# Loading the last two V tiles of a decode attention kernel in quarters

## The chip, the cores and the metric

The kernel runs on one core of a Trainium2 chip. The metric is the device time of one execution in microseconds (us). All runs quoted were in the fast state that the measuring reports. Inside that state the kernel before still shows two groups of times, which the experiments explain.

## The reference

One query per head attends to 8192 keys: 16 heads, head size 256, all in bf16.

```python
B, H, Sq, Sk, D = 1, 16, 1, 8192, 256
scores = jnp.einsum("bhqd,bhkd->bhqk", q, k) * D ** -0.5
p = softmax(scores, axis=-1)
out = jnp.einsum("bhqk,bhkd->bhqd", p, v)
```

K and V are 134 MB together (2 x 16 x 8192 x 256 x 2 bytes), and each byte is used once.

## The kernel before

Each partition holds 64 consecutive rows of K or V of a head, so a tile is [128, 64, 256] and one load is 4 MB. VectorE (DVE) and ScalarE (ACT) compute the scores from K. GpSimd (POOL) takes the maximum across partitions, ACT the exponential, and TensorE (PE) accumulates 64 matmuls with V, one for each row of a partition. After each head come "fill" matmuls whose result nobody reads: they keep PE busy.

```python
KV_BUFS=(3, 3), K_AHEAD=2, NV_CHUNKS_LAST=1, N_FILL=45, N_FILL_LAST=58
...
for h in range(H):
    if h + K_AHEAD < H:
        issue_k(h + K_AHEAD)
    vt = vpool.tile([P, NJ, D], bf16, name=f"vt{h}", tag="vt")
    nvc = NV_CHUNKS_LAST if h == H - 1 else 1
    vstep = (NJ + nvc - 1) // nvc
    for c in range(0, NJ, vstep):
        ce = min(NJ, c + vstep)
        nc.sync.dma_start(out=vt[:, c:ce, :], in_=v_r[h][:, c:ce, :])
    ...                                   # scores, maximum, exponential -> p_sb, lsum
    for j in range(NJ):                   # "value matmuls": oacc
        nc.tensor.matmul(oacc[:, :], lhsT=p_sb[:, j : j + 1], rhs=vt[:, j, :],
                         start=(j == 0), stop=(j == NJ - 1))
    nc.tensor.matmul(ssum[:, :], lhsT=ones_col[:], rhs=lsum[:])
    nfill = N_FILL_LAST if h == H - 2 else (N_FILL if h < H - 1 else 0)
    ...                                   # nfill matmuls of 512 columns: fill
```

The build sets the order on an engine, and it is not that of the source. In the trace of before, for instance, the fills of head 14 start at 294.74 us, the value matmuls of head 13 at 307.38 and those of head 14 at 316.15.

## Time and profile before

| | before |
|---|---|
| time, median (16 runs) | 341.15 us (339.4 to 341.6) |
| span of the profiled execution | 339.4 us |
| bytes read | 135.27 MB, 399 GB/s over the span |
| PE busy / DVE busy | 81% / 83% |

The first lines are from the page of the kernel before. PEclk is the clock granted to PE in tenths of full speed and DMA the busy share of the 16 DMA engines, each in 40 slices of the span; the last line is an issue group: line, queue, number of issues, size, median time from issue to landing.

```profile
PEclk9999958999999999999999999999999999999979
DMA  8999999999999999999999999999999999999300
...
vt<-in_v_dram SPq DMA_DIRECT2D x16, 4096.0 KB, 44.8
```

The DMA row is at 9 from slice 2 to slice 37 of 40 (421 to 450 GB/s): the kernel is bound by its loads, except in the last three slices. There the PEclk row drops to 7. (The 5 in slice 6 is there before PE has its first value matmuls, at 54.2 us here.) All 16 loads of V are single ones of 4 MB.

The next lines are the timeline of PE at the end: start, duration, engine, line and operation, what it writes and reads, how many, and the idle time before it with what ended it. L178 is the fills, L164 the value matmuls, L172 the sum.

```profile
294.74 12.71 PE L178 MATMUL fill<-qb,p 128*64 128x512 bf16 x58
307.38 7.15 PE L164 MATMUL oacc<-vt,p 128*1 128x256 bf16 x64
315.11 0.19 PE L172 MATMUL ssum<-lsum,ones_col 128*1 128x1 f32 x2 [0.58 <-ACT p L153]
316.15 7.15 PE L164 MATMUL oacc<-vt,p 128*1 128x256 bf16 x64 [0.85 <-DMA vt<-in_v_dram]
325.82 8.77 PE L164 MATMUL oacc<-vt,p 128*1 128x256 bf16 x64 [2.53 <-DMA vt<-in_v_dram]
```

These are heads 13, 14 and 15. The last two wait for V. Head 15 waits 2.53 us and then needs 8.77 us for what takes 7.15 us elsewhere. The next lines give windows of the tail: the window, its length, the busy time and number of instructions of PE, of PE's weight loads, of DVE, ACT and POOL, and in the last three columns the granted clock, the DMA share and GB/s.

```profile
310.00:314.00 4.00, 4.00 (x39) 3.09 (x37) 3.61 (x21) 0.00 (x0) 0.10 (x1) 1.00 0.97 418
318.00:322.00 4.00, 4.00 (x39) 3.09 (x37) 0.00 (x0) 0.00 (x0) 0.00 (x0) 1.00 0.12 49
322.00:326.00 4.00, 1.47 (x14) 0.87 (x13) 0.47 (x1) 0.00 (x0) 0.48 (x1) 0.97 0.04 17
326.00:330.00 4.00, 4.00 (x24) 2.55 (x23) 0.00 (x0) 0.00 (x0) 0.00 (x0) 0.60 0.00 0
```

From 318 us on only two, then less than one of the 16 DMA engines on average still move data (0.12, then 0.04), and PE stands waiting for it. Then the clock is 0.60 while the last head is computed.

### The profile page before, as it was taken

How to read it: one execution, taken by the hardware profiler on the slowest of the kernel's cores; microseconds unless marked ns; L12 is line 12 of the kernel's file. 1: busy time of each engine (PE TensorE's matmuls, PEld its weight loads, DVE VectorE, ACT ScalarE, POOL GpSimd, SP SyncE). 2: the span in 40 equal slices, each digit the busy share in tenths (PEclk: the TensorE clock that was granted, in tenths of full speed). 3: DMA queues.
4: the chain of work that ended last, by engine and by line, in shares of the span. 5: the costliest groups of instructions: out<-in, count | busy, mean ns of one | idle time of the engine just before them, and what ended most of it. 6: DMA issues, size and time to landing. Idle time of an engine off the chain costs nothing.

```text
span 339.4 us, 5929 instructions
## 1 busy us (share of the span) xinstructions
PE 274.2 (81%) x1744; PEld 162.8 (48%) x1744; DVE 281.3 (83%) x1297; ACT 183.5 (54%) x897; POOL 15.2 (4%) x36
## 2 busy tenths in 40 slices
PE   0008649999998989898989989879889798899874
PEld 0003226556564646455555646446365554556643
DVE  0998999993998989898989999796998969699000
ACT  0938575660937557392919385581927549093000
POOL 0000020100000000000000000000000000000000
PEclk9999958999999999999999999999999999999979
DMA  8999999999999999999999999999999999999300
GB/s 315 450 433 433 432 426 431 426 432 428 421 427 434 430 431 432 428 430 432 432 432 428 429 434 431 433 430 431 434 423 430 432 427 427 432 427 432 164 8 1
DMA packets 5727, 135.64 MB, mean 400 GB/s; under 512 B 1088, under 2 KB 1088, under 8 KB 1088
## 3 DMA queue, kind: packets, MB, share of 16 engines
q1 hardware_dynamic: 5184, 135.27, 93.0%
q8 instruction: 13, 0.21, 0.3%
q14 instruction: 18, 0.15, 0.1%
q0 software_dynamic: 512, 0.01, 0.1%
HBM read 135.27 MB, written 0.01 MB: 399 GB/s over the span
## 4 chain that ended last, share of the span: by engine, by line
DVE 50%; DMA 28%; PE 11%; issue 7%; POOL 1%; ACT 1%; SPq 0%; POOLq 0%; ACTq 0%; DVEq 0%
DVE kt L127 37%; DMA kt<-in_k_dram 28%; DVE kt L112 11%; PE fill L178 7%; PE oacc L164 4%; DVE scores L127 1%; POOL gmx L141 1%; ACT p L153 1%; DVE mx L139 1%; PE ssum L172 1%; DVE rs L90 0%; DVE nbias L145 0%; POOL out_dram L93 0%; POOLq L215 0%; SPq L73 0%
## 5 line engine op out<-in xcount | busy, mean ns | idle before, releaser
L127 DVE CUSTOM_DVE_ANT_0 kt<-kt,qb 128x256 bf16<-128x256 bf16 x592 | 205.8, 413 | 0.0
L119 ACT ACTIVATE kt<-kt 128x256 bf16<-128x256 bf16 x432 | 172.8, 401 | 26.9 <-DVE kt L112 21.1
L178 PE MATMUL fill<-qb,p 128*64 128x512 bf16 x688 | 157.0, 389 | 0.0
L164 PE MATMUL oacc<-vt,p 128*1 128x256 bf16 x1024 | 116.0, 275 | 10.6 <-DMA vt<-in_v_dram 10.6
L178 PEld LDWEIGHTS <-p 128*64 128x64 bf16 x688 | 76.1, 113 | 73.9 <-issue 6.7
L164 PEld LDWEIGHTS <-p 128*1 128x1 bf16 x1024 | 85.3, 85 | 43.1 <-DMA vt<-in_v_dram 13.4
L119 ACT ACTIVATION_READ_ACCUMULATOR kt<-kt 128x1 f32 x432 | 80.5, 186 | 0.0
L112 DVE TENSOR_TENSOR kt<-kt,qb 128x1024 bf16<-128x1024 bf16 (+2 forms) x48 | 62.3, 1343 | 13.7 <-DMA kt<-in_k_dram 13.7
L153 ACT ACTIVATE p<-scores,nbias 128x64 bf16<-128x64 f32 x16 | 5.6, 348 | 96.6 <-DVE nbias L145 67.4
L127 DVE DVE_READ_ACCUMULATOR2_ANT scores<- 128x1 f32 x592 | 45.0, 76 | 0.0
L172 PE MATMUL ssum<-lsum,ones_col 128*1 128x1 f32 x32 | 3.0, 164 | 49.8 <-ACT p L153 49.8
L172 PEld LDWEIGHTS ssum<-lsum,ones_col 128*1 128x1 f32 x32 | 1.4, 81 | 54.5 <-ACT p L153 54.1
L92 DVE TENSOR_SCALAR osb<-oacc,rs 1x256 bf16<-1x256 f32 x16 | 7.5, 470 | 23.7 <-PE oacc L164 23.3
L141 POOL PARTITION_ALL_REDUCE gmx<-mx x16 | 6.9, 431 | 283.6 <-DVE mx L139 283.6
L93 POOL DMA_DIRECT2D out_dram<-osb x16 | 8.1, 508 | 36.8 <-DVE osb L92 35.6
L145 DVE TENSOR_SCALAR nbias<-gmx 128x1 f32<-128x1 f32 x16 | 2.5, 154 | 8.6 <-POOL gmx L141 8.6
L90 DVE RECIPROCAL rs<-ssum 1x1 f32<-1x1 f32 x16 | 2.5, 155 | 5.6 <-PE ssum L172 5.5
L119 ACT ACT_TABLE_LOAD x1 | 1.3, 1283 | 8.1 <-DMA kt<-in_k_dram 8.1
L139 DVE TENSOR_REDUCE mx<-scores 128x1 f32<-128x64 f32 x16 | 3.5, 219 | 1.4
L153 ACT ACTIVATION_READ_ACCUMULATOR p<-scores,nbias 128x1 f32 x16 | 3.0, 186 | 0.0
L61 DVE MEMSET ones_col<- 128x1 f32 x1 | 0.1, 59 | 0.8 <-PEq L204 0.8
L204 POOL MEMSET const-float32-0.0<- 128x1 f32 x1 | 0.1, 98 | 0.2 <-issue 0.2
(3 smaller groups left out, 0.3 us busy)
## 6 DMA issues: line engine op xcount, KB each, us to landing
vt<-in_v_dram SPq DMA_DIRECT2D x16, 4096.0 KB, 44.8
kt<-in_k_dram SPq DMA_DIRECT2D x15, 4096.0 KB, 37.3
kt<-in_k_dram SPq DMA_DIRECT2D x4, 1024.0 KB, 9.9
qb<-in_q_dram SPq DMA_DIRECT2D x1, 1024.0 KB, 4.7
out_dram<-osb POOLq DMA_DIRECT2D x16, 0.5 KB, 6.6
```

Of the source, the lines that this page charges most:

```text
L90: nc.vector.reciprocal(rs[:], ssum[:, :])
L92: nc.vector.tensor_scalar_mul(o_sb[:], oacc[:, :], rs[:])
L93: nc.gpsimd.dma_start(out=out[0, h], in_=o_sb[:])
L112: nc.vector.tensor_tensor(out=kt[:, c0:c1, :], in0=kt[:, c0:c1, :], in1=qbb.to_broadcast([P, c1 - c0, D]), op=MULT,)
L119: nc.scalar.activation(kt[:, j, :], kt[:, j, :], mybir.ActivationFunctionType.Copy, accum_out=scores[:, j : j + 1],)
L127: nc.vector.tensor_tensor_reduce(out=kt[:, j, :], in0=kt[:, j, :], in1=qb[:, h, :], scale=1.0, scalar=0.0, op0=MULT, op1=ADD, accum_out=sc ...
L139: nc.vector.reduce_max(mx[:], scores[:], axis=mybir.AxisListType.X)
L141: nc.gpsimd.partition_all_reduce(gmx[:], mx[:], channels=P, reduce_op=bass_isa.ReduceOp.max)
L153: nc.scalar.activation(p_sb[:], scores[:], mybir.ActivationFunctionType.Exp, bias=nbias[:], scale=scale, accum_out=lsum[:],)
L164: nc.tensor.matmul(oacc[:, :], lhsT=p_sb[:, j : j + 1], rhs=vt[:, j, :], start=(j == 0), stop=(j == NJ - 1),)
L172: nc.tensor.matmul(ssum[:, :], lhsT=ones_col[:], rhs=lsum[:])
L178: nc.tensor.matmul(fill_ps[:, :], lhsT=p_sb[:, 0:NJ], rhs=qb.rearrange("p h d -> p (h d)")[:, 0 : 2 * D], start=True, stop=True,)
```

## The change

The diff adds ragged row ranges, so that some partitions can hold fewer rows than others, with masks and fills for them, and more chunks for the last V loads. Its core, cut:

```diff
-    NV_CHUNKS_LAST=1,
+    NV_CHUNKS_LAST=4,
+    NK_CHUNKS_FIRST=4,
     N_FILL=45,
     N_FILL_LAST=58,
+    RAGGED=False,
...
+    if RAGGED and Sk == 8192 and P == 128:
+        ranges = RAGGED_RANGES_8192
+        fills = RAGGED_FILL_8192
+    else:
+        ranges = [(0, P, Sk // P)]
+        fills = []
...
+    def load_tile(t, src, row_chunks=1):
+        ...                      # one DMA for each chunk of rows and each range
...
-        nvc = NV_CHUNKS_LAST if h == H - 1 else 1
...
+        load_tile(vt, v_flat[h], row_chunks=NV_CHUNKS_LAST if h >= H - 2 else 1)
```

With RAGGED left at False, all that remains is that V of heads 14 and 15 comes in four loads of 16 rows per partition (1 MB) instead of one of 4 MB.

More of the change, by code (lines that the diff above doesn't have):

```diff
@@ L10 @@
 MULT_CHUNKS_DEFAULT = (4, 12)
+RAGGED_RANGES_8192 = [
+    (0, 4, 62),
+    (4, 8, 64),
+    (8, 32, 65),
+    (32, 36, 62),
+    (36, 64, 64),
+    (64, 72, 63),
+    (72, 88, 64),
+    (88, 96, 65),
+    (96, 104, 63),
+    (104, 128, 64),
+]
+RAGGED_FILL_8192 = [
+    (0, 4, 62),
+    (0, 8, 64),
+    (32, 36, 62),
+    (32, 64, 64),
+    (64, 72, 63),
+    (64, 88, 64),
+    (96, 104, 63),
+    (96, 128, 64),
+]
 @with_exitstack
@@ L34 @@
     assert Sk % P == 0
-    NJ = Sk // P
     scale = float(D) ** -0.5
-    NA = min(NA, NJ)
+    if RAGGED and Sk == 8192 and P == 128:
[4 more added lines that the diff above has]
+        fills = []
+    assert sum((b - a) * n for a, b, n in ranges) == Sk
+    NJX = max(n for _, _, n in ranges)
+    NA = min(NA, min(n for _, _, n in ranges))
+    row_base = []
+    rb = 0
+    for a, b, n in ranges:
+        row_base.append(rb)
+        rb += (b - a) * n
     fp32 = mybir.dt.float32
@@ L61, with issue_k @@
     nc.vector.memset(ones_col[:], 1.0)
-    k_r = [k[0, h].rearrange("(p j) d -> p j d", p=P) for h in range(H)]
-    v_r = [v[0, h].rearrange("(p j) d -> p j d", p=P) for h in range(H)]
-    kts = [None] * H
-    def issue_k(h, nchunks=1):
-        kts[h] = kpool.tile([P, NJ, D], bf16, name=f"kt{h}", tag="kt")
-        step = (NJ + nchunks - 1) // nchunks
-        for c in range(0, NJ, step):
-            ce = min(NJ, c + step)
-            nc.sync.dma_start(out=kts[h][:, c:ce, :], in_=k_r[h][:, c:ce, :])
+    if fills:
+        maskneg = const.tile([P, NJX], fp32)
+        nc.vector.memset(maskneg[:], 0.0)
+        for pa, pb, r0 in fills:
+            nc.vector.memset(maskneg[pa:pb, r0:NJX], -1.0e30)
+    k_flat = [k[0, h] for h in range(H)]
+    v_flat = [v[0, h] for h in range(H)]
+    def load_tile(t, src, row_chunks=1):
+        for a, b, n in ranges:
+            pass
+        bounds = []
+        if row_chunks > 1:
+            step = (NJX + row_chunks - 1) // row_chunks
+            bounds = list(range(step, NJX, step))
+        for ci in range(len(bounds) + 1):
+            for (a, b, n), rb in zip(ranges, row_base):
+                lo = 0 if ci == 0 else bounds[ci - 1]
+                hi = n if ci == len(bounds) else min(n, bounds[ci])
+                if hi <= lo:
+                    continue
+                src3 = src[rb : rb + (b - a) * n, :].rearrange(
+                    "(p j) d -> p j d", p=b - a
+                )
+                nc.sync.dma_start(out=t[a:b, lo:hi, :], in_=src3[:, lo:hi, :])
+        for pa, pb, r0 in fills:
+            nc.gpsimd.memset(t[pa:pb, r0:NJX, :], 0.0)
+    kts = [None] * H
+    def issue_k(h):
+        kts[h] = kpool.tile([P, NJX, D], bf16, name=f"kt{h}", tag="kt")
+        load_tile(kts[h], k_flat[h], row_chunks=NK_CHUNKS_FIRST if h == 0 else 1)
     for hh in range(min(H, K_AHEAD)):
-        issue_k(hh, nchunks=4 if hh == 0 else 1)
+        issue_k(hh)
     mult_bounds = []
@@ L95 @@
     pending = None
+    qb_flat = qb.rearrange("p h d -> p (h d)")
     for h in range(H):
@@ L99 @@
             issue_k(h + K_AHEAD)
-        vt = vpool.tile([P, NJ, D], bf16, name=f"vt{h}", tag="vt")
-        nvc = NV_CHUNKS_LAST if h == H - 1 else 1
-        vstep = (NJ + nvc - 1) // nvc
-        for c in range(0, NJ, vstep):
-            ce = min(NJ, c + vstep)
-            nc.sync.dma_start(out=vt[:, c:ce, :], in_=v_r[h][:, c:ce, :])
+        vt = vpool.tile([P, NJX, D], bf16, name=f"vt{h}", tag="vt")
+        load_tile(vt, v_flat[h], row_chunks=NV_CHUNKS_LAST if h >= H - 2 else 1)
         kt = kts[h]
-        scores = small.tile([P, NJ], fp32, name=f"scores{h}", tag="scores")
+        scores = small.tile([P, NJX], fp32, name=f"scores{h}", tag="scores")
         qbb = qb[:, h : h + 1, :]
@@ L124 @@
             )
-        for j in range(NA, NJ):
+        for j in range(NA, NJX):
             nc.vector.tensor_tensor_reduce(
@@ L135 @@
                 accum_out=scores[:, j : j + 1],
+            )
+        if fills:
+            nc.vector.tensor_tensor(
+                out=scores[:], in0=scores[:], in1=maskneg[:], op=ADD
             )
@@ L149 @@
             pending = None
-        p_sb = small.tile([P, NJ], bf16, name=f"p{h}", tag="p")
+        p_sb = small.tile([P, NJX], bf16, name=f"p{h}", tag="p")
         lsum = small.tile([P, 1], fp32, name=f"lsum{h}", tag="lsum")
@@ L162 @@
         oacc = psum.tile([1, D], fp32, name=f"oacc{h}", tag="oacc")
-        for j in range(NJ):
+        for j in range(NJX):
             nc.tensor.matmul(
@@ L168 @@
                 start=(j == 0),
-                stop=(j == NJ - 1),
+                stop=(j == NJX - 1),
             )
@@ L172 @@
         nc.tensor.matmul(ssum[:, :], lhsT=ones_col[:], rhs=lsum[:])
+        pending = (h, oacc, ssum)
         nfill = N_FILL_LAST if h == H - 2 else (N_FILL if h < H - 1 else 0)
         if nfill > 0:
-            fill_ps = psum.tile([NJ, 2 * D], fp32, name=f"fill{h}", tag="fill")
+            fill_ps = psum.tile([NJX, 2 * D], fp32, name=f"fill{h}", tag="fill")
             for i in range(nfill):
@@ L179 @@
                     fill_ps[:, :],
-                    lhsT=p_sb[:, 0:NJ],
-                    rhs=qb.rearrange("p h d -> p (h d)")[:, 0 : 2 * D],
+                    lhsT=p_sb[:, 0:NJX],
+                    rhs=qb_flat[:, 0 : 2 * D],
                     start=True,
@@ L184 @@
                 )
-        pending = (h, oacc, ssum)
     if pending is not None:
```

## The prediction

> **What the diff really does.** RAGGED defaults to False and the launch passes no arguments, so the ragged ranges, the mask, the GpSimd memsets and the mask add are dead code: ranges collapse to (0, 128, 64), the same 64 rows per partition. The loads of K (first head in 4 chunks) are as before, and moving `pending` above the fill changes nothing. One live change remains: V of the last two heads (14 and 15) is loaded in four DMAs of 16 rows each (1 MB) instead of one of 4 MB, so their value matmuls can start on the first quarter.
>
> **What bounds the kernel now.** The DMA stream. The page shows 0.9 or more DMA share in slices 1 to 36 at about 430 GB/s; 134 MB cannot be shortened by this change. In the timeline of the end, loads become usable every 9.7 us: the last K at 296.7, V14 at 316.15, V15 at 325.82 (starts of the instructions released by them). So the change can only work on the tail. The DMA share by microsecond shows the tail is one slow ring: after 319 us the share is 0.16 to 0.08, about one of 16 engines, moving one 32 KB packet per 1.21 us until 325.4. [...]
>
> **The tail of PE (timeline).** Value matmuls of head 13 run 307.38 to 314.53, the sum matmul at 315.11, head 14 at 316.15 to 323.30, head 15 at 325.82 to 334.59, then the scaling, the output DMA and the end at 339.4. Head 15 takes 8.77 us instead of 7.15: after the 2.5 us gap the granted clock is 0.5 until about 329. [...]
>
> **After.** On the slow engine the quarters of V15 should land about 2.4 us apart, near 318.7, 321.1, 323.6 and 326. Eight-KB packets (query load, first K) took 309 ns, four of them 1236 against 1213 ns for 32 KB, so an estimated 0.4 us later over both heads. PE then never waits long: head 14 starts near 315.2 (three quarters are there, the fourth arrives at about 316.3), ends near 322.4, and head 15 runs straight on; its last quarter is needed at 327.8, after it has landed. It ends near 329.5. The clock stays at full rate because the 2.5 us gap is gone.
>
> Saving: 2.5 us (gap before head 15) + 1.6 us (half clock) + 0.9 us (earlier start of head 14) = 5.0 us. All of it is on the critical path, and the closing 4.8 us (scaling, output, end) stay. Six more DMA issues at 0.33 us on the SP queue are hidden. The floor is the last landing plus 16 matmuls (1.8 us), 327.8 to 328; so at most about 6.8 us, 2%, can come out.
>
> **Predicted: 335.9 us**, range 334.6 to 337.8. Chances: faster by over 2% 0.07, within 2% 0.90, slower 0.03.
>
> **What would show it.** Right: value matmuls on PE gap-free from 307 to about 329.5, granted clock 1.0 up to there, V of heads 14 and 15 in 1 MB issues, everything before 300 us unchanged, last load landing still near 326. Wrong: a PE gap before the last 16 matmuls, or a clock of 0.5 in the tail.
>
> **What would make it wrong.** The build orders PE's stream: if the quarters draw fills between value matmuls, or shift other work, the tail grows. A later quarter of V15 may wait on an earlier DMA's completion before it is issued, and land late. The slow engine may lag by another amount.

Taking every quarter of V15 to need the slow engine is the author's assumption; in after the quarters do land 2.4 to 2.5 us apart, the last at 326.0, at a DMA share of 0.18 and then 0.06.

## The result, and the profile after

| | before | after |
|---|---|---|
| time, median | 341.15 us (16 runs) | 335.60 us (10 runs, 335.54 to 335.93) |
| span of the profiled execution | 339.4 us | 333.9 us |

The ratio is 0.985, with a 95% interval of 0.9833 to 0.9867. Ratios here are the mean time of one kernel's fast runs over that of the other's of the same rounds, so they are not quite the ratio of the medians. The gain of 1.5% is clear of the noise, but small.

From the page after, the same rows and the issue groups of V:

```profile
PEclk9999959999999999999999999999999999999998
DMA  7999999999999999999999999999999999999910
...
vt<-in_v_dram SPq DMA_DIRECT2D x14, 4096.0 KB, 46.8
vt<-in_v_dram SPq DMA_DIRECT2D x8, 1024.0 KB, 31.4
```

The timeline of PE after; L242 is the fills, L226 the value matmuls, L234 the sum:

```profile
294.56 12.71 PE L242 MATMUL fill<-qb,p 128*64 128x512 bf16 x58
307.19 14.13 PE L226 MATMUL oacc<-vt,p 128*1 128x256 bf16 x128
321.16 0.19 PE L234 MATMUL ssum<-lsum,ones_col 128*1 128x1 f32 x2
321.22 7.15 PE L226 MATMUL oacc<-vt,p 128*1 128x256 bf16 x64
```

The windows of the tail after:

```profile
318.00:322.00 4.00, 4.00 (x41) 3.09 (x39) 0.55 (x2) 0.00 (x0) 0.00 (x0) 1.00 0.18 72
322.00:326.00 4.00, 4.00 (x39) 3.09 (x37) 0.00 (x0) 0.00 (x0) 0.48 (x1) 1.00 0.06 23
```

No line of the timeline has a wait in brackets: from the start of the fills at 294.56 to 328.37 (321.22 + 7.15) PE never stops, and its clock is 1.00. The loads did not become faster: one engine is still moving data between 322 and 326 us (0.06 of 16, on average), and in the raw records of the traces the last load packet ends at 325.5 us, against 325.3 before. Only the work that stood behind it is smaller.

The part before the tail is as it was: the fills of head 14 start at 294.56 against 294.74 before. PE ends at 328.37 instead of 334.59 (325.82 + 8.77), 6.2 us earlier, and the span is 5.5 us shorter.

### The profile page after: what moved, and what is told of

Same layout as the page of the kernel before. It is cut to its first block, busy times and chain, and to the rows that moved or that the text cites. A ratio compares the mean times of both kernels' runs of the same rounds, so it can differ in the third digit from the quotient of the medians.

```text
span 333.9 us, 5935 instructions
## 1 busy us (share of the span) xinstructions
PE 270.5 (81%) x1744; PEld 161.8 (48%) x1744; DVE 281.4 (84%) x1297; ACT 183.5 (55%) x897; POOL 15.2 (5%) x36
## 4 chain that ended last, share of the span: by engine, by line
DVE 51%; DMA 28%; PE 11%; issue 6%; POOL 1%; ACT 1%; SPq 0%; POOLq 0%; ACTq 0%; DVEq 0%
DVE kt L185 37%; DMA kt<-in_k_dram 28%; DVE kt L170 11%; PE fill L242 7%; PE oacc L226 4%; DVE scores L185 1%; POOL gmx L203 1%; ACT p L215 1%; DVE mx L201 1%; PE ssum L234 1%; DVE rs L151 0%; DVE nbias L207 0%; POOL out_dram L154 0%; POOLq L277 0%; SPq L126 0%
## 5 line engine op out<-in xcount | busy, mean ns | idle before, releaser
L242 PE MATMUL fill<-qb,p 128*64 128x512 bf16 x688 | 155.4, 386 | 0.0
L226 PE MATMUL oacc<-vt,p 128*1 128x256 bf16 x1024 | 114.1, 273 | 8.9 <-DMA vt<-in_v_dram 8.9
L242 PEld LDWEIGHTS <-p 128*64 128x64 bf16 x688 | 75.6, 112 | 72.8 <-issue 4.9
L226 PEld LDWEIGHTS <-p 128*1 128x1 bf16 x1024 | 84.8, 84 | 40.0 <-DMA vt<-in_v_dram 11.3
L234 PE MATMUL ssum<-lsum,ones_col 128*1 128x1 f32 x32 | 3.0, 164 | 48.9 <-ACT p L215 48.9
L234 PEld LDWEIGHTS ssum<-lsum,ones_col 128*1 128x1 f32 x32 | 1.4, 81 | 53.4 <-ACT p L215 52.9
```

The lines of the kernel that those rows point to most:

```text
L242: nc.tensor.matmul(fill_ps[:, :], lhsT=p_sb[:, 0:NJX], rhs=qb_flat[:, 0 : 2 * D], start=True, stop=True,)
```

## The experiments

The twelve runs were made in four batches. Each batch has its own runs of the kernel before, and those fell differently into two groups, about 339.3 to 340.0 and about 340.8 to 341.6 us, so ratios of different batches are compared with care and medians are quoted.

| run | what it does | median us | ratio to before |
|---|---|---|---|
| e1_v15_only | only V15 in quarters | 337.54 | 0.9924 |
| e2_v14_only | only V14 in quarters | 341.95 | 1.0055 |
| e3_before_warm | before, gap filled with matmuls | 339.70 | 0.9984 |
| e4_fewer_fills | after, 50 last fills instead of 58 | 335.25 | 0.9853 |
| f1_after_again | after, control | 335.66 | 0.9865 |
| f2_no_early_fills | after, far fewer PE instructions | 336.66 | 0.9885 |
| f3_narrow_fills | after, far more PE instructions | 335.68 | 0.9863 |
| f4_ragged | after with RAGGED=True | 1095.81 | 3.2244 |
| g1_tail_tuned | finer tail | 334.09 | 0.9805 |
| g2_tail_tuned_sync_out | g1, last output from the SP queue | 332.90 | 0.9769 |
| g3_more_dve_instr | after, 336 more DVE instructions | 337.97 | 0.9915 |
| g4_fewer_dve_instr | g2, 224 fewer DVE instructions | 332.31 | 0.9745 |

All twelve gave correct results.

### e1 and e2: which of the two heads carries the gain?

```diff
# e1_v15_only
-row_chunks=NV_CHUNKS_LAST if h >= H - 2 else 1
+row_chunks=NV_CHUNKS_LAST if h >= H - 1 else 1
# e2_v14_only
-row_chunks=NV_CHUNKS_LAST if h >= H - 2 else 1
+row_chunks=NV_CHUNKS_LAST if h == H - 2 else 1
```

> After, with only the last head's V in quarters (V14 one 4 MB load again). Theory A (the gain is the last head's matmuls starting on early quarters, plus the clock kept at full rate, plus a smaller part from head 14): head 14 starts at 316.15 as before, ends 323.3, head 15 runs straight on at full clock and ends near 330.5, so about 337.0 us: 4.1 of the 5.5 us. Rival B (head 14's quarters carry the gain, since they free the PE early): 340 us or more.

> After, with only head 14's V in quarters (V15 one 4 MB load). Theory A: head 14 ends near 321.3 but head 15 still waits for its whole V near 325.8, after a gap of 4.5 us, at half clock: no gain, 341.2 us, and the faster mode of before (339.5) should be gone[...]. Rival B: 337 us or less.

Timeline of PE in e1:

```profile
316.00 14.13 PE L226 MATMUL oacc<-vt,p 128*1 128x256 bf16 x128 [0.94 <-DMA vt<-in_v_dram]
```

Timeline of PE in e2:

```profile
307.18 14.13 PE L226 MATMUL oacc<-vt,p 128*1 128x256 bf16 x128
321.15 0.19 PE L234 MATMUL ssum<-lsum,ones_col 128*1 128x1 f32 x2
325.83 8.57 PE L226 MATMUL oacc<-vt,p 128*1 128x256 bf16 x64 [4.49 <-DMA vt<-in_v_dram]
```

In e1 heads 14 and 15 run as one block of 128 matmuls from 316.00 to 330.13: head 15 has no wait of its own. In e2 head 14 is early, but this only makes head 15 wait longer (4.49 us). Then it pays the slow clock: 8.57 us. e2 gains nothing, and all its four runs, 341.5 to 343.1 us, lie in or above the slower group of before. So rival B falls: quarters of V14 alone are worth nothing. With V15 also in quarters they are worth the 1.9 us between e1 (337.54) and after (335.60 and 335.66, measured in other batches). A piece of work moved earlier pays only if what follows can follow.

### e3: the clock by itself

```diff
+        if h == H - 2:
+            warm_ps = psum.tile([NJ, 2 * D], fp32, name="warm", tag="warm", bufs=1)
+            for i in range(10):
+                nc.tensor.matmul(warm_ps[:, :], lhsT=p_sb[:, 0:NJ],
+                    rhs=vt[:, 0:2, :].rearrange("p j d -> p (j d)"), start=True, stop=True)
```

> Before, with ten extra 512-column matmuls on V14 between the value matmuls of heads 14 and 15 (2.2 us of the 2.5 us gap filled; result unchanged). Tests the clock term by itself. Theory A: head 15 still starts near 325.8 but takes 7.15 instead of 8.77 us: 339.5 us, the same in every run, so the two modes of before (339.4 to 339.9 and 340.8 to 341.6) are the clock in this gap. Rival C (nearly all of the gain is the clock): 336 to 337 us. Rival D (the two modes have another cause): both modes still seen.

Timeline of PE in e3 (L174 is the added work):

```profile
322.99 2.35 PE L174 MATMUL warm<-vt,p 128*64 128x512 bf16 x10
325.61 7.15 PE L164 MATMUL oacc<-vt,p 128*1 128x256 bf16 x64 [0.28 <-DMA vt<-in_v_dram]
```

The last head starts when V15 lands, as before, but takes 7.15 us. All four runs lie between 339.53 and 339.76 us, as the faster group of before does, and none in the slower. Four of the seven runs of before in this batch were in the faster group too, so four in a row could still be chance.

The record settles it: in the 30 runs of before whose mean granted clock is listed, every run of the slower group has 0.971 to 0.980 and every run of the faster one 0.981 to 0.985. So the two groups of before are the clock, and in the profiled run this is the clock after this one gap: about 1.6 us, lost in 11 of the 16 runs of the first set (those of 340.75 us or more). In before and e2 the loss is about the same (8.77 and 8.57 us against 7.15) though the gaps differ in length, and the raw clock records show one stretch of half clock of 3.41 us in both: from 325.76 to 329.17 in before (gap 2.53 us) and from 325.38 to 328.79 in e2 (gap 4.49 us). Since e3 still takes 339.70 us and after 335.6, the rest of the gain is earlier work, and rival C falls too.

The length of the gap alone does not decide it: after and f1 are the same kernel, and near 227 us both have a gap of 2.70 us, which is followed by 8.81 us for 64 matmuls in f1 (PEclk 7 in that slice of its page) and by 7.15 in after (9). What does decide it was not shown.

### e4: what bounds the tail after the change?

```diff
-    N_FILL_LAST=58,
+    N_FILL_LAST=50,
```

> After, with 50 instead of 58 fill matmuls for head 14 (they end 1.75 us earlier, near 305.4). Theory A (the tail of after is bound by PE work that starts when the fills end, 307.19, not by a load): head 13 starts when V13 has landed, estimated 306.3, and the end comes 0.5 to 0.9 us earlier: about 334.9 us; the last quarter of V15 (near 326.1, plus 1.8 us) is then the next bound. Rival E (the tail of after is bound by the last landing already): no change, 335.6.

Timeline of PE in e4:

```profile
306.62 15.88 PE L226 MATMUL oacc<-vt,p 128*1 128x256 bf16 x144 [0.77 <-DMA vt<-in_v_dram]
322.33 0.19 PE L234 MATMUL ssum<-lsum,ones_col 128*1 128x1 f32 x2
322.39 3.65 PE L226 MATMUL oacc<-vt,p 128*1 128x256 bf16 x32
326.54 1.91 PE L226 MATMUL oacc<-vt,p 128*1 128x256 bf16 x16 [0.50 <-DMA vt<-in_v_dram]
```

The fills now end early enough for head 13 to wait for its own V (0.77 us), and the last 16 matmuls wait for the last quarter of V15 (0.50 us). The median is 335.25 us, 0.35 to 0.4 us less than after, which is less than the 0.5 to 0.9 us that theory A expected; the runs (334.98 to 335.51) just overlap those of the control f1 (335.46 to 335.83), and in the profiled run PE ends at 328.45, no earlier than in after. So neither theory A nor rival E is settled by the time. The trace says more: PE work and the last landing bind nearly equally. In after the last quarter of V15 has landed at 325.98 and PE comes to it near 326.6 (an estimate: 321.22 plus 48/64 of 7.15 us).

### f2 and f3: do PE's instructions hold up the slow DMA engine?

One DMA engine ends some 8 us after the bulk (the trace doesn't number the engines; each load is counted as landed in 16 steps, and the last step comes 8.1 us after the eighth for the last load of after). A first theory said that PE's own instructions are fetched through it. f1 is the control of this batch.

```diff
# f2_no_early_fills
-    N_FILL=45, N_FILL_LAST=58,
+    N_FILL=0, N_FILL_LAST=36,
# f3_narrow_fills: for heads 0 to 13, 90 fills of 256 columns
-    N_FILL=45,
+    N_FILL=90,
-    rhs=qb_flat[:, 0 : 2 * D],
+    rhs=qb_flat[:, 0:fw],         # fw = 2 * D if h == H - 2 else D
```

> The change as it is, once more, as the control for the three runs beside it on the same chip: 335.6 us.

> After, with no fill matmuls for heads 0 to 13 and 36 for head 14. Asks why one DMA engine ends 8 us behind the others. Theory S (PE's own instructions are fetched through that engine: queue q8 moved 13 packets of 16 KB, as much as 3442 PE instructions of 64 bytes; at 1.21 us per 32 KB of load a packet costs it about 0.6 us, 7.9 us in all): 2138 PE instructions, 8 or 9 packets, loads usable about 3 us earlier at the end (V13 near 303.6, last quarter of V15 near 323.1), about 332.5 us. Rival T (that engine is slow by itself, whatever PE fetches): V15 still lands near 326.1 and the time is 335 to 336.5 us, since the last fills end early and the PE only waits longer.

> After, with twice as many fills of half the width (90 of 256 columns) for heads 0 to 13: the same PE columns, 4702 PE instructions instead of 3442. Theory S: 18 packets on q8, V15's last quarter about 3 us later (near 329.1), which then bounds the tail: about 338.3 us. Rival T: 13 packets' worth of effect or none, 335.6 us.

The first line is from the page of f2, the second from the page of f3: packets, MB and share of the queue that I took for PE's instruction fetch (13 packets before and after).

```profile
q8 instruction: 8, 0.13, 0.2%
```

```profile
q8 instruction: 18, 0.29, 0.4%
```

The packet counts came as expected, so this queue does follow the number of PE instructions (about 64 bytes for each, worked out under g3). The times did not: f3 is at 335.68 us, the same as the control at 335.66. In the raw records of the trace the last load packet ends 323.8 us after the first load begins in after, 323.9 us in f2 and 323.7 us in f3. Theory S falls: whatever these packets cost, it is not on the engine that ends last.

f2 was slower than the control, 336.54 to 336.82 us in three runs and 335.43 in one. Its last fills end at 304.26, and PE then waits 2.54 us for V13 and needs 17.55 instead of the 15.88 us of e4 for 144 value matmuls, the slow clock again. Without the fills of heads 0 to 13 the mean granted clock fell to 0.80 (0.98 in the control), and yet the time rose by 1.0 us only: before the tail the loads bind and not PE (the DMA row of f2 is at 9 there too), so there the slow clock cost nearly nothing.

### f4: the code that the change brings but does not use

```diff
-    RAGGED=False,
+    RAGGED=True,
```

> After with RAGGED=True, the code that the change brings but does not use: partitions 0 to 3 and 32 to 35 get 62 rows, others 63 to 65, in ten DMAs for each tile. Theory S: [...] the tail is then bound by PE (fills end near 307), so no more than 1 us of it is seen: 334.5 to 336. Against it: 320 small loads, memsets on GpSimd and one more add per head could cost more than that. Rival T: the loads do not land earlier.

Theory S was that the last loads land earlier.

It took 1095.81 us, more than three times as long; my expectation was wrong by far. From the waits of the SP queue in f4: who waited for what, us in total, times, longest.

```profile
SPq L126 <- DMA kt<-in_k_dram: 499.0, 175, 9.7
SPq L126 <- DMA vt<-in_v_dram: 463.0, 185, 7.9
```

The queue that issues the loads waited 360 times for an earlier load to land, against 4 such waits in before. Throughput fell to 123 GB/s. In the raw records exactly 4, 8, 12, 14 or 16 load packets are in flight for 80% of the time, while in before it is 15 to 17 for 96%. Over the run the load queue's packets fill 66.2% of the 16 engines' span, against 93.0% in before (pages). The packets are slower too: one of 32 KB, or 64 rows, took 2.6 us in the median instead of 1.21. An estimate from these figures: 399 GB/s x 66.2/93.0 x 1.21/2.6 = 132 GB/s, near the measured 123. So fewer engines in use and slower packets together can account for nearly the whole time. I made no run that takes the two apart, and why the packets are slower stays open; so does how the rows of a tile are spread over the engines. Whether ragged rows would relieve the late engine can't be told from this run.

### g3 and g4: DVE's instructions

In the raw records of before and of after, ten load packets of 32 KB took 1.87 us instead of 1.21 us, each starting 0.3 us after an 8 KB packet of another queue that the page calls instruction (q14). An instruction has 64 bytes by an estimate from these runs: f3 has 2564 PE instructions more than f2, and q8 moved ten packets of 16 KB more, 63.9 bytes for each. Ten packets of 8 KB are then 1280 instructions, and the page counts 1297 for DVE (the recorded texts say 1299). q14 carries a second series, with load packets of 1.59 us behind it: seven in after, eight in g4, where ACT has 1121 instructions instead of 897.

```diff
# g3_more_dve_instr (the tile is made wider; only element 0 is used)
+        if h < H - 2:
+            for i in range(24):
+                nc.vector.memset(nb[0:1, i + 1 : i + 2], float(i))
# g4_fewer_dve_instr (on top of g2): 34 of 64 rows are summed on ACT
-NA_DEFAULT = 27
+NA_DEFAULT = 34
```

> After, with 24 one-element memsets on DVE per head for heads 0 to 13 (336 instructions, about 60 ns each, placed where DVE waits for K; result unchanged). Asks again why one DMA engine lags, after the PE stream was ruled out. Theory S2: that engine also fetches DVE's instructions (1299 of 64 bytes are ten 8 KB packets on q14; ten load packets of 32 KB took 1.87 instead of 1.21 us right behind one): 2 or 3 packets more, 0.9 us each, V15's last quarter 1.8 to 2.9 us later, about 337.5 us. Rival T (the engine lags whatever is fetched): the last landing stays within 0.4 us and the time is 335.6 to 335.9 us.

> As the tuned version with the output on the SP queue, and with 34 instead of 27 of the 64 rows per partition summed on ACT (NA=34). DVE then has 1075 instead of 1299 instructions, ACT 14 more per head. Theory S2 in the other direction (DVE's instructions are fetched through the engine that lands last): 8 or 9 instead of 10 slow packets of about 1.87 us, last landing 1 to 2 us earlier, and the tail of PE follows it down to the PE bound: 331.0 to 332.2 us against 332.9. Rival T (the lag does not depend on DVE's instructions): the last landing does not move and the time stays at 332.9.

From the raw records (not a view of the profile): load packets of 32 KB that took 1.80 to 1.90 us, and the end of the last load packet after the start of the first:

```
kernel    DVE instructions   slow packets   last load ends, us
after     1297               10             323.8
f2        1297               10             323.9
f3        1297               10             323.7
g3        1633               13             327.2
g2        1297               10             324.5
g4        1073                8             323.2
```

The windows of the tail of g3, in the columns used above:

```profile
318.00:322.00 4.00, 4.00 (x39) 3.08 (x37) 0.21 (x1) 0.23 (x2) 0.50 (x1) 1.00 0.19 76
322.00:326.00 4.00, 4.00 (x41) 3.08 (x39) 0.55 (x2) 0.00 (x0) 0.49 (x1) 1.00 0.06 27
326.00:330.00 4.00, 4.00 (x39) 3.10 (x37) 0.00 (x0) 0.00 (x0) 0.00 (x0) 1.00 0.05 19
```

The bulk ends as in after: the DMA share is 0.19 against 0.18 from 318 to 322 us. The one late engine goes on into 326 to 330 us, where after shows no load. So the added DVE work did not starve the loads. It made the late engine later, by 3.4 us for three packets, and the time rose from 335.6 to 337.97 us.

The landings show the same inside single runs. Each load is counted as landed in 16 steps, and I take the time from the eighth step to the last. In after it grows from 0.3 us at the first load to 8.1 us at the last. It goes up by 0.6 to 1.0 us in each of the ten loads during which one of the ten packets passes, and hardly elsewhere (near 195 us it drops once by 1.1 us, since the eighth step came later). The last value is 11.2 us in g3, 8.3 in g2 and 7.0 in g4.

The time did not follow by the path that was expected. Timeline of PE in g3:

```profile
297.92 12.71 PE L246 MATMUL fill<-qb,p 128*64 128x512 bf16 x58
310.55 14.13 PE L230 MATMUL oacc<-vt,p 128*1 128x256 bf16 x128
324.58 7.15 PE L230 MATMUL oacc<-vt,p 128*1 128x256 bf16 x64
```

No matmul waits for V15. The whole tail starts late, at 297.92 instead of 294.56: the engine that is late for V is late for K too, DVE starts on K of head 14 when it has landed, at 279.5 instead of 276.1, and the fills need the exponential of that head. That is 3.4 us; the stretch after PE was 1.0 us shorter in this profile, and the span is 2.4 us longer.

g4 shows the opposite direction: two slow packets fewer, the last landing 1.2 us earlier than in g2 (323.25 against 324.46), and 332.31 instead of 332.90 us (no overlap: 331.73 to 332.40 against 332.89 to 332.92). In g4 as in g2 PE doesn't wait after the last fills start, so here too the last landing isn't what sets the time; the fills start 0.36 us earlier. g4 also moves work from DVE to ACT, so its gain in time is not only the packets. For the landing theory S2 holds in both directions: ten slow packets and a last landing at 323.8 us with 1297 DVE instructions, thirteen and 327.2 us with 1633; and ten and 324.5 us in g2, eight and 323.2 us with 1073 in g4. That the 8 KB packets fetch DVE's instructions is read from their number, and that they pass on the engine that lands last from the steps of its lag; the trace names neither. Why a packet costs about 1 us there, three times the 0.31 us that 8 KB takes by itself, stays open.

### g1 and g2: a version that beats both

```diff
# g1_tail_tuned
-row_chunks=NV_CHUNKS_LAST if h >= H - 2 else 1
+row_chunks=NV_CHUNKS_LAST if h >= H - 3 else 1,
+cuts=[16, 32, 48, 56] if h == H - 1 else None
-N_FILL_LAST=58
+N_FILL_LAST=50
# g2_tail_tuned_sync_out, on top of g1
-        nc.gpsimd.dma_start(out=out[0, h], in_=o_sb[:])
+        eng = nc.sync if h == H - 1 else nc.gpsimd
+        eng.dma_start(out=out[0, h], in_=o_sb[:])
```

> A version meant to beat both: V of head 13 in quarters too, V15 in pieces of 16, 16, 16, 8 and 8 rows, 50 fills for head 14. If the tail is now bound by the landing of V15's last piece (e4 showed a 0.5 us wait there), only 8 matmuls (0.9 us) instead of 16 stand behind it, and PE, which starts head 13 without waiting for all of V13, has caught up by then: PE ends near 327.1 instead of 328.4, about 334.4 us. If PE work is still the bound, 335.0 to 335.3, as e4.

> As the run before, with the last head's output written by a DMA from the SP queue instead of GpSimd. The closing stretch from the last scaling to the end of the span was 5.5 us in after. If the GpSimd queue's start is part of it, 0.3 to 1 us is saved: about 333.8 us. If it is only the write's completion and the end of the program, no change against the run before.

The end of the timeline of all engines in g1:

```profile
327.81 0.47 DVE L153 TENSOR_SCALAR osb<-oacc,rs 1x256 bf16<-1x256 f32 x1 [6.51 <-PE oacc L227]
328.58 0.48 POOL L154 DMA_DIRECT2D out_dram<-osb  x1 [6.49 <-DVE osb L153]
```

And in g2:

```profile
328.11 0.47 DVE L153 TENSOR_SCALAR osb<-oacc,rs 1x256 bf16<-1x256 f32 x1 [6.51 <-PE oacc L228]
328.61 0.31 SPq L155 DMA_DIRECT2D out_dram<-osb  x1
```

g1 took 334.09 us, 1.5 us less than after, near the 334.4 expected, but not only by the expected path. PE ends at 327.78, 0.6 us earlier than in after and not the expected 1.3; the build put 23 of the 50 fills between the quarters of heads 13 and 14, the risk that the prediction of the change had named, and PE has no wait from 294.65 on. The other 1.0 us of the profiles' difference is the stretch from the end of PE to the end of the span, 4.5 us here and 5.5 in after, which g1 doesn't touch.

In g2 the issue follows the last scaling by 0.03 us instead of 0.30, and the span (331.1 us) ends 2.5 us after the issue starts instead of 3.7 us (span 332.3). The time fell by a further 1.2 us to 332.90, slightly more than expected. In the raw records it is 0.74 us in g2 and 1.05 in g1 from the start of the issue to the first packet of the output. The larger part of the gain lies after the last packet of the output: the span ends 1.75 us after it in g2 and 2.51 in g1.

g4, with 332.31 us and a ratio of 0.9745 (0.972 to 0.977), is the fastest.

## Why the prediction was right

- **The landings of V15's quarters**: right. Predicted near 318.7, 321.1, 323.6 and 326; counted as landed at 318.6, 321.0, 323.5 and 326.0 in after.
- **What the diff does**: right. Only V of heads 14 and 15 changed, in eight issues of 1 MB.
- **The bound**: right. The loads fill the time to about 318 us in both kernels, and only the tail moved.
- **The gap before head 15, 2.5 us**: right. It is gone, and e1 and e2 show that the quarters of V15 remove it.
- **The half clock, 1.6 us**: right in size, measured alone by e3. The prediction took it as a cost of every run; it was in 11 of 16.
- **Head 14, 0.9 us**: too small. The build moved the sum of head 15 behind the matmuls of head 14, so that heads 13 and 14 run as one block and head 15 starts at 321.22 instead of near 322.4. The prediction named the build's order as a risk; here it helped, by 1.1 us.
- **The closing stretch, 4.8 us**: too small in the other direction. After takes 5.5 us from the end of PE to the end of the span (333.9 - 328.4). The two misses nearly cancel, so that 335.9 came so close to 335.6 is in part luck. The stretch isn't fixed: apart from f4, the eleven profiles whose last output goes through GpSimd have 4.5 to 5.5 us, and f1, which is the same kernel as after, has 5.25. So its length can't be put down to the change. What it depends on I did not find; g2 shows that the path of the last output is a part of it.
- **A late issue of a V15 quarter**: it happened and cost nothing. The last issue of V in after starts at 306.25 us, when V13, whose semaphore it reuses, had landed (306.24), and the data was still in time.
- **The slow engine** was taken as given. What the runs show of its lateness: its lag grows from 0.3 to 8.1 us in steps of 0.6 to 1.0 us, one for each of the ten 8 KB packets whose number follows DVE's instructions, and it is 11.2 us with thirteen of them (g3) and 7.0 with eight (g4, against 8.3 with ten in g2).

## What to carry to other kernels

When loads bind the whole run, look at what stands behind the last landing: cut the last loads finely enough that only a small piece of work waits for the final bytes, and keep the engine that needs them busy until just before they come (in f2 its fills end too early, and the time was 1.0 us longer). Moving one step earlier gains nothing if the step behind it still waits (e2), and an idle gap near the end can be paid twice, as here with 2.5 us of waiting and 1.6 us of lower clock. A DMA share of about one sixteenth at the end of a load stream meant one late engine here (0.06 from 322 to 326 us), and it can pay to ask what else that engine carries. Its lag was not a matter of the end alone: it grew over the whole run, from 0.3 to 8.1 us, and in g3 K of head 14 came 3.4 us later as the last V did.
